# Scores in one product of 128 keys, and the forward table built ahead of the first casts: a windowed attention and spectral-mixing kernel on one core

## The chip, the cores and the metric

The kernel runs on one NeuronCore of a Trainium2 chip. The core has five engines that run side by side, each with its own instruction stream: TensorE (PE in the profile; its weight loads have a row of their own, PEld), VectorE (DVE), ScalarE (ACT), GpSimd (POOL) and SyncE (SP). Transfers between HBM and the on-chip memory SBUF are carried by 16 DMA engines; here they are issued by GpSimd, which can also cast float32 to bfloat16 on the way, and by SyncE. Matrix products land in PSUM, a small memory of eight banks.

The metric is the device time of one launch in microseconds (us); lower is better. Three runs of the kernel before took 447.45, 447.73 and 449.92 us, so the median is 447.73 us.

## What is computed

The reference has two parts, one fed into the other:

```python
# attention: batch 8, heads 8, seq 576, head_dim 64, window 64
scores = scale * np.matmul(q, k.transpose(0, 1, 3, 2))
rel = pos[:, None] - pos[None, :]
scores = np.where((rel >= 0) & (rel < 64), scores, -1000000000.0)
attn = softmax(scores)                      # max taken off first
x = np.matmul(attn, v)                      # then to [8, 576, 512]

# spectral mixing: the 64 lowest modes of a real FFT over the sequence
X = np.fft.rfft(x, axis=1)[:, :64]
Yr = einsum('bmd,mde->bme', Xr, w_r) - einsum('bmd,mde->bme', Xi, w_i)
Yi = einsum('bmd,mde->bme', Xr, w_i) + einsum('bmd,mde->bme', Xi, w_r)
u = x + np.fft.irfft(Y, n=576, axis=1)
out = u + np.maximum(u @ w_ch, 0.0)
```

A query sees itself and the 63 keys before it. So a block of 64 queries, number n, needs only the 128 keys of blocks n - 1 and n, and block 0 only its own 64. Each of the 64 modes has its own 512 x 512 matrices w_r and w_i, float32 in HBM; they are cast to bfloat16 by the DMA that loads them.

## The kernel before

**Stages.** The attention of all batches runs first and takes up the time to about 195 us. Meanwhile GpSimd already loads the weights of the modes, as far as there is room, and the first ten groups of four modes are multiplied for half of the features (`early_step`, L454). Then the remaining modes are multiplied as their weights arrive, while TensorE fits in the product of x and w_ch. A last stage brings the modes back to positions and writes the output.

**Attention.** A group g is four heads of one batch; there are 16. For each, q, k and v arrive as [128, 18, 64] tiles `rawq`, `rawk`, `rawv` (two buffers each). `transpose_raw` (L208) turns half a tile by 18 small transposes on TensorE into a PSUM tile `tr`, and ScalarE copies that to `qT`, `kT` or `vT` (L218). The `tr` tiles, and the tiles `vb` of `place_v`, share two PSUM buffers. `place_v` (L221) transposes v back, so that keys lie on partitions, and writes it into `vd` by VectorE: slot n of `vd` holds the 128 key rows that block n needs, in the order in which the columns of its scores stand. Odd slots are written from PSUM (L229), the even ones are put together out of the odd ones (L232, L233).

**Units.** 40 units of up to eight tiles [128 x 128] follow one another in a software pipeline (loop at L467, `it` from -3 to 42). `do_s` (L246) starts a PSUM tile `s` of four score tiles with the mask (L253, a product with the identity), adds the products of q and k, and takes the row maximum on VectorE (L271). `do_exp` takes the maximum off with one more product (L279) and exponentiates on ScalarE (L281); `do_pt` transposes the result (L287), and `do_pv` multiplies it with `vd` (L307) and divides by the row sum.

In `do_s`, an odd block n has its 128 keys in the order previous, own, which is the order in `kT`, and takes one product of 128 columns (L261). An even block has them in the order own, previous, and takes two products of 64 columns (L264, L267); block 0 takes only its own. Each product has its own weight load. The mask `mask_t` has three layouts: [0] for units with an even and an odd block, [1] the same with nothing before block 0, [2] for units that hold block 8 alone.

**Order of the loads.** GpSimd issues in program order. The loads of k and q of group g + 2 (L201) wait until the transposes of the group before in that buffer are done; the loads of weights (L155) stand between them, and how many are issued in each step is fixed by `due(it)` (L451).

**The start.** SyncE loads k and q of group 0 without a cast, and VectorE casts them (L348). GpSimd makes the identity (masks.py), loads v of group 0, and after two iotas the loads of group 1, two more iotas (`at`, L369 and L371), and the first weights. VectorE makes the masks and, behind them, the argument of the forward table (cosines and sines for the transform to modes): seven steps on [128 x 384] (L400 to L407). ScalarE takes the sine, between two loads of its function tables (Sin, then Exp), in step `it` = -1 (`forward_table`, L410; called at L478), after the first six copies of `tr`. Q, R and `at` lie in a tile (`XQ`) that is used for weights and modes later. The table `trigF` is first read by the transforms of step 7 (`do_dft`).

Of the kernel before, what the change touches and what calls it, by code (L numbers as in the profile page):

```python
# [11 lines left out]
BF16 = mybir.dt.bfloat16  # L12

ALU = mybir.AluOpType
ACT_F = mybir.ActivationFunctionType
# [5 lines left out]
NEG = -1.0e30  # L21
# [5 lines left out]
def kernel(  # L27
# [10 lines left out]
    nc = tc.nc  # L38
    B, H, S, D = q.shape
# [26 lines left out]
    ident = consts.tile([128, 128], FP32, name="ident")  # L66
    ident_bf = consts.tile([128, 128], BF16, name="ident_bf")
# [111 lines left out]

    with tc.manual_schedule():  # L180
        maskp = pool("maskp")
        mask_t = maskp.tile([128, 3, 4, 128], BF16, name="mask_t")
        rawp = pool("rawp", bufs=2)
        qtp = pool("qtp", bufs=3)
        vtp = pool("vtp")
# [11 lines left out]
        def load(g, nm):  # L197
            hb, b = divmod(g, B)
            src = {"q": q, "k": k, "v": v}[nm][b, 4 * hb:4 * hb + 4]
            r = rawp.tile([128, TP, D], BF16, name="raw" + nm, tag="raw" + nm)  # L200
            nc.gpsimd.dma_start(out=r, in_=src.rearrange("h (p j) d -> (h p) j d", j=TP))  # L201
            raws[g, nm] = r
# [18 lines left out]
        def place_v(g, pr):  # L221
            vd, t = Vd[g % NVD], turned[g, "v"][:, pr]
            pt = ps_m.tile([128, NTC, 2, D], BF16, name="vb", tag="misc")
            for c in range(NTC):
                n = min(128, S - 128 * c)
                nc.tensor.transpose(out=pt[0:n, c].rearrange("p h d -> p (h d)"), in_=t[:, 128 * c:128 * c + n],  # L226
                                    identity=ident_bf)
            hd = slice(pr, 4, 2)
            nc.vector.tensor_copy(out=vd[:, 1:9:2, hd, 0:D], in_=pt[:, 0:4])  # L229
            nc.vector.tensor_copy(out=vd[0:64, 8, hd, 0:D], in_=pt[0:64, 4])  # L230
            if pr:
                nc.vector.tensor_copy(out=vd[0:64, 0:8:2, :, 0:D], in_=vd[0:64, 1:9:2, :, 0:D])  # L232
# [13 lines left out]
        def do_s(u, c2):  # L246
            g0, cc, tl = units[u]
            if c2 >= len(tl) // 4:
                return
            s = ps_s.tile([128, 4, 128], FP32, name="s")  # L250
            st[u]["s", c2] = s
            mk = 2 if cc == 2 else (1 if (cc == 0 and c2 == 0) else 0)
            nc.tensor.matmul(out=s, lhsT=ident_bf, rhs=mask_t[:, mk], start=True, stop=True)  # L253
            for t, g, pr, n in tl[4 * c2:4 * c2 + 4]:
                t -= 4 * c2
                qT, kT = turned[g, "q"][:, pr], turned[g, "k"][:, pr]
                for hh in range(2):
                    ro = slice(64 * hh, 64 * hh + 64)
                    lq = qT[ro, 64 * n:64 * n + 64]
                    if n % 2:  # L260
                        nc.tensor.matmul(out=s[ro, t, :], lhsT=lq, rhs=kT[ro, 64 * n - 64:64 * n + 64],  # L261
                                         start=False, stop=True, skip_group_check=True)
                    else:
                        nc.tensor.matmul(out=s[ro, t, 0:64], lhsT=lq, rhs=kT[ro, 64 * n:64 * n + 64],  # L264
                                         start=False, stop=True, skip_group_check=True)
                        if n:
                            nc.tensor.matmul(out=s[ro, t, 64:128], lhsT=lq, rhs=kT[ro, 64 * n - 64:64 * n],  # L267
                                             start=False, stop=True, skip_group_check=True)
# [90 lines left out]
        nc.gpsimd.iota(Pcol, pattern=[[0, 1]], base=0, channel_multiplier=1,  # L359
                       allow_small_or_imprecise_dtypes=True)  # L360
        nc.gpsimd.iota(Kf, pattern=[[1, 64]], base=0, channel_multiplier=0,
                       allow_small_or_imprecise_dtypes=True)
        for nm in ("k", "q", "v"):
            load(1, nm)
        scratch = XQ[1].rearrange("p s b m -> p (s b m)").bitcast(FP32)
        Q = scratch[:, 0:NTF * 2 * NM].rearrange("p (c a m) -> p c a m", c=NTF, a=2)
        R = scratch[:, NTF * 2 * NM:3 * NTF * NM].rearrange("p (c m) -> p c m", c=NTF)
# [2 lines left out]
                       allow_small_or_imprecise_dtypes=True)  # L370
        nc.gpsimd.iota(at[:, NTC:NTF], pattern=[[0, 1]], base=128 * (NTC - 1) - 64, channel_multiplier=1,  # L371
                       allow_small_or_imprecise_dtypes=True)
        LEAD = 4
# [6 lines left out]
        ve.tensor_single_scalar(out=Gcol, in_=Pcol, scalar=64.0, op=ALU.is_ge)  # L380
        ve.scalar_tensor_tensor(out=Mcol, in0=Gcol, scalar=-64.0, in1=Pcol, op0=ALU.mult, op1=ALU.add)
        curm = mask_t[:, 0, 0, 0:64]
        prvm = mask_t[:, 0, 0, 64:128]
        ve.tensor_scalar(out=curm, in0=Kf, scalar1=Mcol, scalar2=NEG, op0=ALU.is_gt, op1=ALU.mult)
        ve.tensor_scalar(out=prvm, in0=Kf, scalar1=Mcol, scalar2=NEG, op0=ALU.is_le, op1=ALU.mult)
        for f in casts:
            f()
        for i in range(NVD):
            nc.gpsimd.memset(Vd[i][:, :, :, D:D + 1], 1.0)
            nc.gpsimd.memset(Vd[i][64:128, 0, :, :], 0.0)  # L390
        ve.tensor_copy(out=mask_t[:, 0, 1, 0:64], in_=prvm)
        ve.tensor_copy(out=mask_t[:, 0, 1, 64:128], in_=curm)
        ve.tensor_copy(out=mask_t[:, 0, 2:4, :], in_=mask_t[:, 0, 0:2, :])
        ve.tensor_copy(out=mask_t[:, 1], in_=mask_t[:, 0])
        ve.memset(mask_t[:, 1, 0:4:2, 64:128], NEG)
        ve.tensor_copy(out=mask_t[:, 2, 0:4:2, :], in_=mask_t[:, 0, 0:4:2, :])
        ve.tensor_copy(out=mask_t[:, 2, 1:4:2, :], in_=mask_t[:, 0, 0:4:2, :])
        ve.tensor_copy(out=ident_r, in_=ident)
        turns = Q[:, :, 1, :]
        ve.scalar_tensor_tensor(out=turns, in0=Kf.unsqueeze(1).to_broadcast([128, NTF, NM]), scalar=1.0 / S,  # L400
                                in1=at.unsqueeze(2).to_broadcast([128, NTF, NM]), op0=ALU.mult, op1=ALU.mult)
# [5 lines left out]
        ve.tensor_scalar(out=turns, in0=turns, scalar1=-PSAFE / (2.0 * np.pi), scalar2=PSAFE / (2.0 * np.pi),  # L407
                         op0=ALU.max, op1=ALU.min)

        def forward_table():  # L410
            nc.scalar.preload_act_table(ACT_F.Sin)
            nc.scalar.activation(out=trigF.rearrange("p c (a m) -> p c a m", a=2), in_=Q, func=ACT_F.Sin,
                                 scale=-2.0 * np.pi)
            nc.scalar.preload_act_table(ACT_F.Exp)

        def trig_steps():
            yield lambda: ve.memset(trigF[64:128, NTC - 1, :], 0.0)
# [49 lines left out]
        for it in range(-3, NU + 3):  # L467
            todo = tq.get(it, [])
            reshape(todo[0:1])
            if 0 <= it < NU:  # L470
                do_exp(it)
            if 0 <= it + 1 < NU:
                do_s(it + 1, 0)
            reshape(todo[1:2])
            if 0 <= it + 1 < NU:
                do_s(it + 1, 1)
            if it == -1:
                forward_table()  # L478
# [12 lines left out]
            reshape(todo[3:])  # L491

            g = starts.get(it + 2)
            if g is not None and g + 2 < NG:
                load(g + 2, "k")
                load(g + 2, "q")
            g = starts.get(it + 1)
            if g is not None and g + 2 < NG:
                load(g + 2, "v")
            if it >= 0:  # L500
                for f in trig[0:2]:
                    f()
                del trig[0:2]
            load_weights(due(it) - loaded())
# [338 lines left out]
```

## Time and profile before

| | us |
|---|---|
| median of three runs (447.45 to 449.92) | 447.73 |
| the profiled execution, its own time | 445.86 |
| its span, from the first to the last instruction | 444.1 |

| engine | busy us | share of the span |
|---|---|---|
| TensorE products | 337.2 | 76% |
| TensorE weight loads | 217.6 | 49% |
| VectorE | 216.3 | 49% |
| ScalarE | 173.8 | 39% |
| GpSimd | 143.4 | 32% |

The profile comes from one execution that a hardware profiler recorded. A row of a group or of the timeline has the line of the kernel, the engine and operation, what is written and read (out<-in, by tile names) and the size. In the timeline the first two numbers are the start from the begin of the span and the duration; a bracket at the end says how long the engine had stood idle before and what released it. In the chain of waits the work that ended last is followed back, at each step to what released it; "issue" there and as a releaser means that nothing in the profile explains the wait. "Granted clock" is the share of TensorE's full clock that it was given in a stretch. The share of the DMA engines can go over 1.00, since the times of packets overlap a little. A busy TensorE isn't TensorE at its peak, since its products overlap.

### The profile page before, as it was taken

What the parts mean: (1) busy time and instruction counts of PE and PEld (TensorE: products, weight loads), DVE (VectorE), ACT (ScalarE), POOL (GpSimd) and SP (SyncE); (2) the same over time, 40 slices, a digit from 0 to 9 for tenths busy, and PEclk for the clock granted to TensorE, in tenths of its full rate; (3) what the DMA queues carried; (4) which work ended last, traced back from release to release, by engine and by line L of the source; (5) the groups of instructions that cost most, each with busy time, mean ns of one, the idle gap of its engine ahead of it and who ended that gap; (6) DMA issues with size and microseconds to landing.
All of it is one profiled execution on the core that took longest, in us unless ns stands there. A gap on an engine that the chain in (4) does not pass through costs nothing.

```text
span 444.1 us, 11428 instructions
## 1 busy us (share of the span) xinstructions
PE 337.2 (76%) x4926; PEld 217.6 (49%) x4968; DVE 216.3 (49%) x448; ACT 173.8 (39%) x305; POOL 143.4 (32%) x211
## 2 busy tenths in 40 slices
PE   7687988888899988896317555775778576698994
PEld 4466766665676756674114222443344343353552
DVE  5576777765667666677204111212123122344773
ACT  4665756564575756641202100111122121123662
POOL 9242423221425243232232323132233222300773
PEclk9899999998999999999758656869889968889998
DMA  8999999999999999999999999999999999992787
GB/s 211 210 211 211 212 212 209 211 211 211 170 211 148 210 211 211 211 212 211 211 258 211 211 211 211 211 211 211 211 211 211 211 211 211 211 197 61 268 297 270
DMA packets 47875, 93.48 MB, mean 211 GB/s; under 512 B 3536, under 2 KB 3664, under 8 KB 47824
## 3 DMA queue, kind: packets, MB, share of 16 engines
q0 software_dynamic: 42000, 81.73, 98.1%
q1 hardware_dynamic: 5824, 11.01, 7.3%
q8 instruction: 39, 0.64, 0.5%
q14 instruction: 12, 0.10, 0.1%
HBM read 163.58 MB, written 9.44 MB: 390 GB/s over the span
## 4 chain that ended last, share of the span: by engine, by line
PE 41%; DMA 40%; issue 10%; ACT 4%; POOL 1%; DVE 1%; DVEq 0%; SPq 0%; POOLq 0%; ACTq 0%
DMA wr<-in_moe_w_r_dram 36%; PE tr L214 7%; PE s L279 4%; PE pt L287 4%; PE vb L226 4%; PE s L264 3%; DMA wi<-in_moe_w_i_dram 3%; PE o L307 3%; PE s L253 2%; PE psm L171 2%; PE s L261 2%; DMA vd<-in_q_dram 1%; PE px L330 1%; ACT vT L218 1%; POOL wi L155 1%
## 5 line engine op out<-in xcount | busy, mean ns | idle before, releaser
L593 PE MATMUL psz<-wch,tr 128*128 128x512 f32 x176 | 65.4, 505 | 11.0 <-DMA wch<-in_moe_w_ch_dram 11.0
L669 DVE CAST xw<-psz 128x512 fp32r<-128x512 f32 x36 | 24.9, 692 | 95.7 <-PE psz L593 94.2
L155 POOL DMA_DIRECT2D wi<-in_moe_w_i_dram x62 | 44.1, 712 | 84.4 <-PE psm L171 57.3
L271 DVE TENSOR_REDUCE mx<-s 128x4 fp32r<-128x512 f32 x72 | 49.7, 691 | 35.8 <-PE s L261 29.7
L171 PEld LDWEIGHTS <-XQ 128*32 128x32 bf16 x512 | 23.6, 168 | 84.9 <-issue 78.5
L155 POOL DMA_DIRECT2D wr<-in_moe_w_r_dram x53 | 38.1, 718 | 76.0 <-PE psm L171 37.5
L570 ACT CAST tr<-ptx 128x512 fp32r<-128x512 bf16 x36 | 21.2, 588 | 101.5 <-PE ptx L586 101.5
L171 PE MATMUL psm<-wi,XQ 128*32 128x512 bf16 x244 | 32.6, 451 | 34.1 <-DMA wi<-in_moe_w_i_dram 34.1
L593 PEld LDWEIGHTS psz<-wch,tr 128*128 128x128 f32 x176 | 38.6, 243 | 17.4 <-issue 11.3
L171 PE MATMUL psm<-wr,XQ 128*32 128x512 bf16 x212 | 29.0, 468 | 23.0 <-DMA wr<-in_moe_w_r_dram 22.3
L281 ACT ACTIVATE p<-s 128x512 bf16<-128x512 f32 x72 | 39.8, 604 | 15.2 <-PE s L279 15.2
L218 ACT COPY kT<-tr 128x576 bf16<-128x576 bf16 x32 | 23.2, 724 | 29.4 <-PE tr L214 29.4
L264 PE MATMUL s<-kT,qT 64*64 64x64 bf16 x320 | 25.7, 204 | 8.1 <-issue 8.1
L201 POOL DMA_DIRECT2D rawk<-in_k_dram x15 | 8.3, 555 | 70.3 <-PE tr L214 70.3
L768 POOL TENSOR_TENSOR ut<-ut,XQ 128x512 f32<-128x512 f32 x16 | 20.6, 1285 | 28.1 <-DVE ut L752 21.8
L218 ACT COPY qT<-tr 128x576 bf16<-128x576 bf16 x32 | 23.3, 729 | 11.0 <-PE tr L214 11.0
L290 DVE COPY pts<-pt 128x1024 bf16<-128x1024 bf16 (+1 forms) x40 | 25.3, 632 | 3.7 <-PE pt L287 1.9
L279 PE MATMUL s<-mx,ident_r 128*128 128x512 f32 x72 | 26.9, 447 | 0.0
L218 ACT COPY vT<-tr 128x576 bf16<-128x576 bf16 x32 | 23.3, 730 | 7.0 <-PE tr L214 6.9
L261 PE MATMUL s<-kT,qT 64*64 64x128 bf16 x256 | 23.6, 225 | 2.7 <-issue 2.7
L264 PEld LDWEIGHTS <-qT 64*64 64x64 bf16 x320 | 15.5, 109 | 20.7 <-issue 20.3
L287 PE MATMUL pt<-ident_bf,p 128*128 128x128 bf16 x288 | 23.0, 220 | 0.2 <-DVE pts L290 0.2
(180 smaller groups left out, 630.0 us busy)
## 6 DMA issues: line engine op xcount, KB each, us to landing
wi<-in_moe_w_i_dram POOLq DMA_DIRECT2D x60, 512.0 KB, 15.7
wr<-in_moe_w_r_dram POOLq DMA_DIRECT2D x53, 512.0 KB, 16.4
out_dram<-ut SPq DMA_DIRECT2D x32, 256.0 KB, 2.3
rawv<-in_v_dram POOLq DMA_DIRECT2D x16, 288.0 KB, 11.1
rawk<-in_k_dram POOLq DMA_DIRECT2D x15, 288.0 KB, 9.4
rawq<-in_q_dram POOLq DMA_DIRECT2D x15, 288.0 KB, 9.8
Ypair<-in_moe_w_r_dram POOLq DMA_DIRECT2D x5, 512.0 KB, 12.7
x_sb<-in_moe_w_r_dram POOLq DMA_DIRECT2D x4, 512.0 KB, 12.4
```

The lines of the kernel that those rows point to most:

```text
L155: nc.gpsimd.dma_start(out=w[:, 0:len(ps)], in_=src[ps[0]:ps[-1] + 1, HALF * hb:HALF * hb + HALF, :].rearrange("g (p j) e -> p g j e", j=NJ))
L171: nc.tensor.matmul(out=psm[32 * g:32 * g + 32, :], lhsT=XQ[hb].rearrange("k s b m -> k (s b) m")[:, (3 * j + 1 - ri) * B:(3 * j + 5 - ri) ...
L214: nc.tensor.transpose(out=pt[ro, j, :], in_=raw[ro, TH * half + j, :], identity=ident_bf[ro, ro])
L218: nc.scalar.copy(out=to, in_=pt.rearrange("p j n -> p n j"))
L261: nc.tensor.matmul(out=s[ro, t, :], lhsT=lq, rhs=kT[ro, 64 * n - 64:64 * n + 64], start=False, stop=True, skip_group_check=True)
L264: nc.tensor.matmul(out=s[ro, t, 0:64], lhsT=lq, rhs=kT[ro, 64 * n:64 * n + 64], start=False, stop=True, skip_group_check=True)
L271: nc.vector.tensor_reduce(out=mx, in_=s, axis=AX.X, op=ALU.max, negate=True)
L279: nc.tensor.matmul(out=s, lhsT=ident_r, rhs=mx.unsqueeze(2).to_broadcast([128, 4, 128]), start=False, stop=True, skip_group_check=True)
L281: nc.scalar.activation(out=p[:, 4 * c2:4 * c2 + 4, :], in_=s, func=ACT_F.Exp, scale=EX_SCALE)
L287: nc.tensor.transpose(out=pt[:, t, :], in_=st[u]["p"][:, t, :], identity=ident_bf)
L290: nc.vector.tensor_copy(out=ps[:, 0:nt, :], in_=pt[:, 0:nt, :])
L593: nc.tensor.matmul(out=pz, lhsT=tr[:, c, :], rhs=wch[:, c, :], start=(c == 0), stop=(c == NDCH - 1))
```

## The change

- Scores: every block n > 0 takes one product of 128 columns, keys in the order previous, own. Block 0 writes columns 64 to 127. 256 products and their 256 weight loads go.
- v: the even slots of `vd` are put together with their halves exchanged, so the copies move rows from partitions 0 to 63 to 64 to 127, and the other way. The zeros for the block before the first one stand in the lower half.
- Masks: one order for all units, so two layouts in place of three, and fewer steps to make them.
- Forward table: its iotas (Kf and the two of `at`) stand first on GpSimd, ahead of the identity and of all loads; its seven steps stand first on VectorE, ahead of the casts of k and q, with the cast of the identity among them; the sine with its two loads of function tables stands ahead of the first copy on ScalarE, and no longer in step -1.
- The masks and `ident_r` are made behind the casts.

```diff
-        mask_t = maskp.tile([128, 3, 4, 128], BF16, name="mask_t")
+        mask_t = maskp.tile([128, 2, 4, 128], BF16, name="mask_t")
...
-            nc.vector.tensor_copy(out=vd[0:64, 8, hd, 0:D], in_=pt[0:64, 4])
+            nc.vector.tensor_copy(out=vd[64:128, 8, hd, 0:D], in_=pt[0:64, 4])
             if pr:
-                nc.vector.tensor_copy(out=vd[0:64, 0:8:2, :, 0:D], in_=vd[0:64, 1:9:2, :, 0:D])
-                nc.vector.tensor_copy(out=vd[64:128, 2:9:2, :, 0:D], in_=vd[64:128, 1:9:2, :, 0:D])
+                nc.vector.tensor_copy(out=vd[64:128, 0:8:2, :, 0:D], in_=vd[0:64, 1:9:2, :, 0:D])
+                nc.vector.tensor_copy(out=vd[0:64, 2:9:2, :, 0:D], in_=vd[64:128, 1:9:2, :, 0:D])
...
-            mk = 2 if cc == 2 else (1 if (cc == 0 and c2 == 0) else 0)
+            mk = 1 if cc == 0 and c2 == 0 else 0
...
-                    if n % 2:
-                        nc.tensor.matmul(out=s[ro, t, :], lhsT=lq, rhs=kT[ro, 64 * n - 64:64 * n + 64],
-                                         start=False, stop=True, skip_group_check=True)
-                    else:
-                        nc.tensor.matmul(out=s[ro, t, 0:64], lhsT=lq, rhs=kT[ro, 64 * n:64 * n + 64],
-                                         start=False, stop=True, skip_group_check=True)
-                        if n:
-                            nc.tensor.matmul(out=s[ro, t, 64:128], lhsT=lq, rhs=kT[ro, 64 * n - 64:64 * n],
-                                             start=False, stop=True, skip_group_check=True)
+                    lo = 64 if n == 0 else 0
+                    nc.tensor.matmul(out=s[ro, t, lo:128], lhsT=lq, rhs=kT[ro, 64 * n - 64 + lo:64 * n + 64],
+                                     start=False, stop=True, skip_group_check=True)
...
         casts = list(load_by_sp(0, "k", Vflat[1])) + list(load_by_sp(0, "q", Vflat[2]))
-        masks.make_identity(nc, ident)
-        load(0, "v")
-        nc.gpsimd.iota(Pcol, ...)
         nc.gpsimd.iota(Kf, ...)
-        for nm in ("k", "q", "v"):
-            load(1, nm)
...
         nc.gpsimd.iota(at[:, 0:NTC], ...)
         nc.gpsimd.iota(at[:, NTC:NTF], ...)
+        masks.make_identity(nc, ident)
+        load(0, "v")
+        nc.gpsimd.iota(Pcol, ...)
+        for nm in ("k", "q", "v"):
+            load(1, nm)
         LEAD = 4
         load_weights(LEAD)
...
-        ve.tensor_copy(out=ident_bf, in_=ident)
-        (Gcol, Mcol, curm, prvm, the casts, the copies of the masks, ident_r)
         ve.scalar_tensor_tensor(out=turns, ...)
         ve.tensor_scalar(out=R, in0=turns, scalar1=MAGIC, scalar2=None, op0=ALU.add)
+        ve.tensor_copy(out=ident_bf, in_=ident)
...
-        def forward_table():
-            nc.scalar.preload_act_table(ACT_F.Sin)
-            nc.scalar.activation(out=trigF..., in_=Q, func=ACT_F.Sin, scale=-2.0 * np.pi)
-            nc.scalar.preload_act_table(ACT_F.Exp)
+        nc.scalar.preload_act_table(ACT_F.Sin)
+        nc.scalar.activation(out=trigF..., in_=Q, func=ACT_F.Sin, scale=-2.0 * np.pi)
+        nc.scalar.preload_act_table(ACT_F.Exp)
+        (Gcol, Mcol)
+        for f in casts:
+            f()
+        (the ones and zeros of vd, by GpSimd)
+        ve.tensor_copy(out=ident_r, in_=ident)
+        (the masks: curm, prvm, three copies, one memset)
...
-            if it == -1:
-                forward_table()
```

More of the change, by code (lines that the diff above doesn't have):

```diff
@@ L408 @@
                          op0=ALU.max, op1=ALU.min)
-        def forward_table():
[L411 to L414, printed above, removed]
+        nc.scalar.preload_act_table(ACT_F.Sin)
+        nc.scalar.activation(out=trigF.rearrange("p c (a m) -> p c a m", a=2), in_=Q, func=ACT_F.Sin,
+                             scale=-2.0 * np.pi)
+        nc.scalar.preload_act_table(ACT_F.Exp)
+        ve.tensor_single_scalar(out=Gcol, in_=Pcol, scalar=64.0, op=ALU.is_ge)
+        ve.scalar_tensor_tensor(out=Mcol, in0=Gcol, scalar=-64.0, in1=Pcol, op0=ALU.mult, op1=ALU.add)
+        for f in casts:
+            f()
+        for i in range(NVD):
+            nc.gpsimd.memset(Vd[i][:, :, :, D:D + 1], 1.0)
+            nc.gpsimd.memset(Vd[i][0:64, 0, :, :], 0.0)
+        ve.tensor_copy(out=ident_r, in_=ident)
+        prvm, curm = mask_t[:, 0, 0, 0:64], mask_t[:, 0, 0, 64:128]
+        ve.tensor_scalar(out=curm, in0=Kf, scalar1=Mcol, scalar2=NEG, op0=ALU.is_gt, op1=ALU.mult)
+        ve.tensor_scalar(out=prvm, in0=Kf, scalar1=Mcol, scalar2=NEG, op0=ALU.is_le, op1=ALU.mult)
+        ve.tensor_copy(out=mask_t[:, 0, 1, :], in_=mask_t[:, 0, 0, :])
+        ve.tensor_copy(out=mask_t[:, 0, 2:4, :], in_=mask_t[:, 0, 0:2, :])
+        ve.tensor_copy(out=mask_t[:, 1], in_=mask_t[:, 0])
+        ve.memset(mask_t[:, 1, 0:4:2, 0:64], NEG)
         def trig_steps():
```

23 lines of the change are left out of this document (2 added, 21 removed).

## The prediction, made before the changed kernel had run

> **What bounds the kernel now.** I read the page first, then the busy time by stages with the DMA rate, then the order of time on GpSimd, and last the chain of waits through the first 30 us.
>
> ```profile
> span 444.1 us, 11428 instructions
> PE 337.2 (76%) x4926; PEld 217.6 (49%) x4968; DVE 216.3 (49%) x448; ACT 173.8 (39%) x305; POOL 143.4 (32%) x211
> q0 software_dynamic: 42000, 81.73, 98.1%
> q8 instruction: 39, 0.64, 0.5%
> ```
>
> No engine is full, but the queue of the loads that GpSimd issues is: its packets take 98.1% of all 16 DMA engines. So the question is where those engines run dry. The stages show it (columns: stretch, its length, busy time and count of PE, PEld, DVE, ACT, POOL, then granted clock, DMA share, GB/s):
>
> ```profile
> 15.00:20.00 5.00, 3.10 (x25) 1.79 (x25) 1.55 (x4) 3.14 (x5) 0.00 (x0) 0.74 1.12 209
> 105.00:110.00 5.00, 4.62 (x75) 3.22 (x69) 2.46 (x6) 2.53 (x4) 0.00 (x0) 0.66 1.12 211
> 110.00:120.00 10.00, 8.62 (x189) 6.37 (x190) 6.70 (x17) 5.79 (x12) 4.46 (x7) 1.00 1.00 165
> 134.00:145.00 11.00, 10.50 (x238) 7.56 (x241) 8.44 (x21) 6.30 (x12) 5.89 (x9) 1.00 0.89 146
> 145.00:195.00 50.00, 45.29 (x1044) 33.72 (x1053) 33.68 (x74) 30.54 (x55) 15.54 (x23) 1.00 1.12 211
> 195.00:387.00 192.00, 121.81 (x857) 67.91 (x858) 52.59 (x99) 33.53 (x61) 53.64 (x75) 0.78 1.12 214
> ```
>
> The rate is 211 GB/s nearly everywhere up to the last weight, whatever the engines do, and 165 and 146 GB/s in two holes. The holes cost 10 x (211 - 165)/211 = 2.2 us and 11 x (211 - 146)/211 = 3.4 us: 5.6 us in which the stream stood. After 145 us it never stands again, and the last weights end the stage:
>
> ```profile
> 388.28 13.64 DMA wi<-in_moe_w_i_dram
> ```
>
> They land at 401.9 us; what follows is untouched by the change. So the end moves only by what the two holes lose or gain. GpSimd makes the holes:
>
> ```profile
> 124.17 0.56 POOL L201 DMA_DIRECT2D rawk<-in_k_dram  x1 [7.30 <-PE tr L214]
> ...
> 136.30 0.53 POOL L201 DMA_DIRECT2D rawk<-in_k_dram  x1 [6.46 <-PE tr L214]
> ```
>
> Each load of k waits until TensorE has transposed the previous k out of that buffer, and the weights are queued behind it. When TensorE is late in the attention stage, GpSimd issues late, and the DMA engines empty what they had. If TensorE is earlier by some lead at 111 and 136 us, these issues come earlier by it, while the stream that begins at 1 to 2 us is the same. The time lost is then 5.6 us minus the lead, not below nothing. So I sum the lead.
>
> **The forward table's sine, moved ahead of the copies: 2.6 us of lead.** In the chain of waits ScalarE holds TensorE up, because the two table loads and the sine stand ahead of a copy of k that frees a PSUM buffer:
>
> ```profile
> 12.30 1.28 ACT L411
> 13.60 0.84 ACT trigF L412
> 14.46 1.28 ACT L414
> 15.75 0.73 ACT kT L218
> 16.52 0.56 PE vb L226 x5
> ...
> 12.41 0.69 PE L214 MATMUL tr<-ident_bf,rawk 64*64 64x64 bf16 x18
> ```
>
> Without the three, the copy waits only for its transposes, until 12.41 + 0.69 = 13.10. It ends at 13.85 and vb starts at 13.9 instead of 16.52: 2.6 us.
>
> What they pass on the way costs something at the start:
>
> ```profile
> 0.74 0.20 POOL masks.py:197 MEMSET ident<- 128x128 f32 x1 [0.29 <-POOLq L827]
> 1.20 5.17 DMA vd<-in_q_dram
> 3.96 0.19 POOL L369 IOTA XQ<- 128x5 f32 x1
> 5.03 0.94 DVE L348 CAST rawk<-vd 128x576 bf16<-128x576 f32 x2 [1.83 <-DMA vd<-in_k_dram]
> 6.35 0.72 ACT L218 COPY kT<-tr 128x576 bf16<-128x576 bf16 x1 [4.33 <-PE tr L214]
> 7.74 0.67 PE L214 MATMUL tr<-ident_bf,rawk 64*64 64x64 bf16 x18
> 9.44 0.54 DVE L400 SCALAR_TENSOR_TENSOR XQ<-Kf,XQ 128x384 f32<-128x384 f32 x1
> 12.30 0.36 DVE L407 TENSOR_SCALAR XQ<-XQ 128x384 f32<-128x384 f32 x1
> ```
>
> On GpSimd three iotas of at most 0.2 us go ahead of the identity and the first loads, so v's first load is issued some 0.4 us later and the weights, behind all of it in both kernels, not at all. That is hidden: k and q, by SyncE, keep the DMA engines full till 6.37. On VectorE the seven table steps took 9.44 to 12.66, 3.2 us. From about 1.3 (0.74 plus the iotas) with the identity's cast and two one-column steps (an estimate: 0.2 each, from the 0.36 of L407) they end near 5.2, against 5.03 for k's first cast: 0.2 us late. ScalarE's sine then runs at about 4.9 and Exp's table is in at 7.0, so the first copy of k comes 0.65 later than 6.35 and ends at 7.7. Its buffer is wanted by the next transposes of k, which start at 7.74 behind q's, and q lands at 6.37 anyway: cost 0, with 0.05 us of cover; a later table costs its whole delay. I allow 0 to 1.5 us. The masks, now shorter by three copies, end near 9.6 and are wanted at 9.96.
>
> **The half-clock stretch after that pause: 1.0 us.** In 15 to 20 us the granted clock is 0.74, so 1.3 us of clock is missing right behind TensorE's 2.9 us pause. With the pause gone I take 1.0 (TensorE is busy 3.10 of those 5 us, so not all of it counts); bounds 0 and 1.7, the latter from 105 to 110, where (1 - 0.66) x 5 is missing.
>
> **One product of 128 keys: 0.4 us.** A warm block of scores:
>
> ```profile
> 24.10 0.22 PE L264 MATMUL s<-kT,qT 64*64 64x64 bf16 x2
> 24.15 0.20 PE L267 MATMUL s<-kT,qT 64*64 64x64 bf16 x2
> 24.18 0.23 PE L261 MATMUL s<-kT,qT 64*64 64x128 bf16 x2
> 24.24 0.20 PE L264 MATMUL s<-kT,qT 64*64 64x64 bf16 x2
> ```
>
> From start to start a pair of 64 columns takes 0.03 to 0.05 and a pair of 128 takes 0.06: the streaming is equal, and only the odd 0.00 to 0.02 per block is saved. Some 50 of the 72 blocks stand ahead of 136 us: 0 to 1.0, I take 0.4.
>
> **512 fewer PE instructions: 0.6 us.** 4926 + 4968 instructions in 39 transfers of q8 are 254 for each, so two transfers go. TensorE pauses in the middle of equal transposes, with nothing to wait for:
>
> ```profile
> PE tr L214 <- issue: 5.8, 6, 1.8
> ```
>
> I read these as instructions not yet there, about 1 us each; not every transfer has one. Two transfers fewer, three quarters of them ahead of 136 us: 0 to 2.9 (1.5 x 1.9) better, and up to 1 worse since the pauses fall elsewhere; I take 0.6. The Trainium skill (Runtime: NRT & Kernel Launch, Instruction fetch mechanics) says that fetching is mostly hidden; by that rule this term is 0 and the lead 4.0. The pauses inside one group speak against it here.
>
> **v, placed to match: 0.** The copies now move 64 partitions up or down:
>
> ```profile
> L232 DVE COPY vd<-vd 64x1024 bf16<-64x1024 bf16 x16 | 6.7, 418 | 0.0
> L794 DVE CAST zst<-psz 128x512 fp32r<-128x512 f32 x1 | 0.7, 692 | 1.4 <-PE psz L788 1.4
> L800 DVE CAST Z<-psp 16x512 fp32r<-16x512 f32 x1 | 0.7, 682 | 0.5 <-PE psp L799 0.5
> ```
>
> L800 writes rows 96 to 111 from rows 0 to 15 and costs what L794 does in place. So the count is the same and I take no change; at worst, at L800's 1.33 ns per element, a copy costs 1.37 instead of 0.42, all on VectorE, which is idle over a quarter of this stage. The Trainium skill (VectorE: DVE Perf Modes, Two Vector instructions with no wait between them) says that an instruction whose output starts in another 32-partition group than the last is held until all earlier ones end; by it these copies lose an overlap that is under 0.1 us each, off the path, and the sum stays.
>
> **Sum.** 2.6 + 1.0 + 0.4 + 0.6 = 4.6 us of lead at 136 us, so the holes keep 1.0 of their 5.6 us. The loads allow that lead at their tightest place:
>
> ```profile
> rawk<-in_k_dram POOLq DMA_DIRECT2D x15, 288.0 KB, 9.4
> 21.44 0.55 POOL L201 DMA_DIRECT2D rawk<-in_k_dram  x1 [8.22 <-PE tr L214]
> 35.48 0.45 PE L214 MATMUL tr<-ident_bf,rawk 64*64 64x64 bf16 x18
> ```
>
> 21.44 + 9.4 = 30.8 is 4.6 us ahead of its use, where the lead is 3.6 to 3.8. The profiled execution took 445.86 us (span 444.1 and 1.76 around it) and would take 441.3; the median of the runs is 1.87 above it, so 447.73 - 4.6 = 443.1.
>
> **Rivals.** *All of both holes goes:* the half-clock stretch at 105 to 110, behind another pause, doesn't recur; the lead grows by up to 1.7 and the gain stops at 5.6: 442.1. For it: the pauses move. Against: some pause may fall as badly. The Trainium skill (TensorE: Matmul & The Clock Gate, Part 1) says that the clock is judged in free-running windows, so chance decides; that is why this stays a rival. *The lead is spent:* TensorE, now earlier, catches up with its loads, pauses there, and gets two half-clock stretches of 1.7 us ahead of 136 us: 4.6 - 3.4 = 1.2, so 446.5. For it: only 0.8 to 1.0 us of margin at that k. Against: in the rows the wait runs the other way, GpSimd for TensorE. *Slower, by the table at the start:* the VectorE steps, beside GpSimd's descriptors and memsets, take three times 3.2 us. The first cast waits 6.4 us more, all attention with it, and 6.6 - 4.6 = 2.0 us is lost: 449.7. It decides once the steps take over 3.2 + 4.4 = 7.6 us. Against: at 9.44 they ran beside four loads' issues too. *The merged product saves nothing:* 443.5, inside the forecast.
>
> **How the numbers follow.** Forecast 0.48, all holes gone 0.18, lead spent 0.20, slower 0.14. About 0.5%, 2.2 us, can be told from no change here: below 445.5 is faster, above 450.0 slower by it; under the last case I count the worse starts too. Faster: 0.44 + 0.18 + 0.04 = 0.66; same: 0.04 + 0.15 + 0.02 = 0.21; slower: 0.01 + 0.12 = 0.13. The range goes from 441.3 (all gone, less 0.8 for scatter) to 447.6 (lead spent, plus 1.1); the likeliest alone has 442.1 to 444.8.
>
> **What would show it.** Right: first vb near 13.9 us; no clock below 0.9 in 15 to 20; over 200 GB/s in the first hole and over 190 in what is left of the second; last weights at about 397.3; span near 439.5. Wrong in a step: the first copy of k after 7.7; score blocks of the same length but more pauses between; copies of v over 0.5 us; TensorE waiting for DMA ahead of transposes. Wrong altogether: the holes filled and the end not moved, or the lead there and the holes as deep.

## The result, and the profile after

| | before | after |
|---|---|---|
| median of the runs, us | 447.59 (446.12 to 449.92, 4 runs) | 442.51 (441.96 to 443.10, 4 runs) |
| the profiled execution, its own time | 445.86 | 441.96 |
| its span | 444.1 | 440.2 |
| last weights land | 401.92 | 397.02 |

The ratio of the times is 0.9882, with a 95% interval from 0.9837 to 0.9927: 5.1 us less from median to median, where the prediction had 4.6. The two profiled executions stand 3.9 us apart. The rest is scatter of the kernel before: its median lies 1.7 us above its profiled execution, that of the changed kernel 0.55 above.

The head of the page of the changed kernel, in the same rows as before:

```profile
span 440.2 us, 10911 instructions
PE 330.7 (75%) x4670; PEld 211.8 (48%) x4712; DVE 219.8 (50%) x445; ACT 172.8 (39%) x304; POOL 143.3 (33%) x211
q0 software_dynamic: 42000, 81.73, 98.4%
q8 instruction: 37, 0.61, 0.5%
```

The same bytes in the load queue, 256 products and 256 weight loads fewer, and two instruction transfers fewer. The stages of the changed kernel (stretch, length, busy time and count of PE, PEld, DVE, ACT, POOL, granted clock, DMA share, GB/s):

```profile
1.00:8.00 7.00, 4.15 (x30) 1.49 (x32) 6.74 (x15) 3.49 (x4) 6.86 (x16) 1.00 0.90 237
15.00:20.00 5.00, 4.39 (x63) 2.65 (x63) 2.90 (x8) 1.68 (x4) 0.20 (x1) 0.63 1.12 211
105.00:110.00 5.00, 3.95 (x77) 2.93 (x71) 2.50 (x5) 2.78 (x8) 1.95 (x3) 1.00 1.12 211
110.00:120.00 10.00, 9.52 (x213) 6.91 (x218) 7.20 (x15) 6.56 (x12) 3.24 (x5) 1.00 1.12 212
134.00:145.00 11.00, 10.61 (x266) 8.54 (x269) 7.48 (x15) 8.15 (x17) 3.71 (x6) 1.00 1.12 211
383.00:397.00 14.00, 10.56 (x59) 5.24 (x59) 4.46 (x8) 2.34 (x4) 0.83 (x2) 0.90 0.88 164
394.00:402.00 8.00, 7.03 (x21) 2.62 (x21) 1.38 (x2) 0.64 (x2) 0.00 (x0) 0.57 0.14 26
```

And the stretches of the kernel before that stand against the first and the last two of them: the start, the same 14 us ahead of the last landing, and the 8 us around it:

```profile
1.00:8.00 7.00, 5.04 (x54) 2.35 (x56) 3.64 (x12) 1.77 (x3) 6.73 (x15) 1.00 0.90 243
388.00:402.00 14.00, 11.37 (x64) 6.66 (x62) 4.46 (x8) 2.34 (x4) 0.83 (x2) 0.82 0.91 171
398.00:406.00 8.00, 5.18 (x26) 2.05 (x21) 1.57 (x3) 0.83 (x2) 0.00 (x0) 1.00 0.20 38
```

Both holes are gone altogether: 212 and 211 GB/s where 165 and 146 stood. That is the whole 5.6 us. Three smaller things take some of it back:

- The stream starts a little later: 237 against 243 GB/s from 1 to 8 us, which is 6 x 7 / 211 = 0.2 us.
- It thins out a little more at its end: 164 against 171 GB/s in the 14 us ahead of the last landing, 7 x 14 / 211 = 0.5 us. So the last weights land 5.6 - 0.2 - 0.5 = 4.9 us earlier, which is what the chain of waits of the changed kernel shows:

```profile
383.28 13.74 DMA wi<-in_moe_w_i_dram
397.07 1.01 PE psm L171 x2
```

- From there to the end it takes 440.2 - 397.0 = 43.2 us instead of 42.2. The products behind the last weights take 1.01 us where they took 0.61, since the granted clock from 394 to 402 us is 0.57; in the kernel before it is 1.00 around its last landing.

5.6 - 0.2 - 0.5 - 1.0 = 3.9 us, the distance of the two spans.

**The lead of TensorE** is read at the loads of k on GpSimd, which wait for its transposes. The rows that stood at 111.36 and 136.30 us before are, in the timeline of the changed kernel:

```profile
102.61 0.55 POOL L201 DMA_DIRECT2D rawk<-in_k_dram  x1 [2.95 <-PE tr L214]
127.25 0.53 POOL L201 DMA_DIRECT2D rawk<-in_k_dram  x1 [5.90 <-PE tr L214]
```

They are 8.8 and 9.0 us earlier, twice the 4.6 that were forecast. The start doesn't give this. The chain of waits of the changed kernel at its place:

```profile
13.80 0.73 ACT kT L218
14.58 0.83 PE vb L226 x5
```

vb starts at 14.58 instead of 16.52, 1.9 us earlier. The other 7 us come later, in the attention loop. What TensorE waits for there can be read in the view of waits: the releaser, then total us, count and longest. First the kernel before, from 20 us to the load of k at 136; then the changed kernel from 18 us to the same load at 127 (three rows with a named releaser, 1.8 us in all and the same in both, are left out):

```profile
PE tr L214 <- issue: 5.5, 5, 1.8
PE s L264 <- issue: 4.5, 26, 0.4
PE vb L226 <- issue: 1.0, 1, 1.0
PE s L261 <- issue: 1.0, 2, 0.6
PE o L307 <- issue: 0.9, 1, 0.9
```

```profile
PE s L261 <- issue: 4.1, 25, 0.3
PE tr L214 <- issue: 1.7, 4, 0.9
PE pt L281 <- issue: 1.3, 2, 0.8
PE vb L226 <- PE o L301: 0.7, 1, 0.7
PE vb L226 <- issue: 0.2, 1, 0.2
```

The rows marked "issue" sum to 12.9 and 7.3 us. The many short ones, 0.16 us each ahead of a product of q and k, are nearly alike in both (4.5 and 4.1 us). The few long ones, for which the profile names nothing that TensorE waited for, have shrunk. The row of 0.7 us that the profile puts down to a product belongs with them: this pause, at 43.87 us, sits where the long ones sit, 510 recorded instructions behind the one at 31.79 us (see below). With it the pauses went from 12.9 to 8.0 us, 4.9 us less. With 1.9 from the start, and 1.7 from the half clock at 105 to 110 us that didn't come back (0.66 before, 1.00 now), less 0.5 for 15 to 20 us, where it is 0.63 instead of 0.74, that makes 8.0 of the 9.0 us; the last 1.0 us isn't accounted for.

### The profile page after: what moved, and what is told of

Its sections match the earlier page's. It is cut to its first block, busy times and chain, and to the rows that moved or that the text cites. A ratio compares the mean times of both kernels' runs of the same rounds, so it can differ in the third digit from the quotient of the medians.

```text
span 440.2 us, 10911 instructions
## 1 busy us (share of the span) xinstructions
PE 330.7 (75%) x4670; PEld 211.8 (48%) x4712; DVE 219.8 (50%) x445; ACT 172.8 (39%) x304; POOL 143.3 (33%) x211
## 4 chain that ended last, share of the span: by engine, by line
DMA 42%; PE 40%; issue 8%; DVE 3%; ACT 3%; POOL 1%; DVEq 0%; POOLq 0%
DMA wr<-in_moe_w_r_dram 35%; PE tr L214 6%; PE s L261 5%; PE s L273 4%; PE pt L281 4%; PE vb L226 4%; DMA rawk<-in_k_dram 4%; DMA wi<-in_moe_w_i_dram 3%; PE psm L171 3%; PE o L301 3%; PE s L253 2%; PE psm L720 1%; PE px L324 1%; PE pst L746 1%; PE psz L720 1%
## 5 line engine op out<-in xcount | busy, mean ns | idle before, releaser
L579 PE MATMUL psz<-wch,tr 128*128 128x512 f32 x176 | 61.4, 480 | 11.0 <-DMA wch<-in_moe_w_ch_dram 11.0
L171 PE MATMUL psm<-wi,XQ 128*32 128x512 bf16 x244 | 34.2, 453 | 39.9 <-DMA wi<-in_moe_w_i_dram 39.9
L171 PE MATMUL psm<-wr,XQ 128*32 128x512 bf16 x212 | 27.9, 448 | 27.3 <-DMA wr<-in_moe_w_r_dram 26.7
L579 PEld LDWEIGHTS psz<-wch,tr 128*128 128x128 f32 x176 | 35.9, 226 | 16.8 <-issue 11.2
L261 PE MATMUL s<-kT,qT 64*64 64x128 bf16 (+1 forms) x576 | 29.4, 223 | 6.9 <-issue 6.9
L261 PEld LDWEIGHTS <-qT 64*64 64x64 bf16 x576 | 18.0, 108 | 18.4 <-issue 17.9
L598 DVE TENSOR_TENSOR stg<-psm,Ypair 128x512 bf16<-128x512 f32 x10 | 6.9, 690 | 35.1 <-PE psm L171 35.1
L313 DVE TENSOR_TENSOR x_sb<-o,r 128x512 bf16<-128x512 f32 x32 | 22.1, 691 | 1.1
```

What stands on the lines that cost most here:

```text
L171: nc.tensor.matmul(out=psm[32 * g:32 * g + 32, :], lhsT=XQ[hb].rearrange("k s b m -> k (s b) m")[:, (3 * j + 1 - ri) * B:(3 * j + 5 - ri) ...
L261: nc.tensor.matmul(out=s[ro, t, lo:128], lhsT=lq, rhs=kT[ro, 64 * n - 64 + lo:64 * n + 64], start=False, stop=True, skip_group_check=True)
L579: nc.tensor.matmul(out=pz, lhsT=tr[:, c, :], rhs=wch[:, c, :], start=(c == 0), stop=(c == NDCH - 1))
```

## What the long pauses are: the question for the experiments

The packets of the instruction queue (q8) that fall into attention begin, taken from the two traces, at

```
before  60.2 66.2 72.1 78.1 84.0 90.0 96.0 102.4 108.3 113.5 121.5 127.5 133.4 137.2 144.1
after   59.4 65.3 71.3 77.2 83.2 89.3 95.2 101.0 107.1 113.4 119.7 125.7 131.6 137.9 143.8
```

and carry 16 KB each, by the prediction's division some 254 PE instructions. They come 5.8 to 6.1 us apart nearly everywhere, whatever TensorE runs. In the stretch from 20 to 140 us the view of DMA counts for the kernel before

```profile
q8 instruction: 20, 0.33, 1.0%
```

and the same 20 for the changed one, and TensorE's own row there is, before and after,

```profile
20.00:140.00 120.00, 104.75 (x2540) 0.98 1.09 203
```

```profile
20.00:140.00 120.00, 109.58 (x2507) 1.00 1.12 211
```

About the same number of products in the same time, though those of the second are longer. With as many weight loads that is 42 instructions per us, and 254 in 5.95 us is 43. So the reading is: while the DMA engines are full of loads, TensorE gets its next block of instructions only every 5.95 us, and a stage with many small instructions goes at that pace. 512 instructions fewer in the 195 us of attention are then 512 / 42 = 12 us of supply, not the 0.6 of the prediction. This is theory F in the expectations below. Against it stands the prediction's own reading, that the start brings most of the lead and fetching next to nothing, and as a third the possibility that the new place of v and the masks bring it.

## The experiments

### The scores alone

The kernel before, with the one product per block, v and the masks as in the change, and the old start:

```diff
...
+                    lo = 64 if n == 0 else 0
+                    nc.tensor.matmul(out=s[ro, t, lo:128], lhsT=lq, rhs=kT[ro, 64 * n - 64 + lo:64 * n + 64], ...)
...
-                nc.vector.tensor_copy(out=vd[0:64, 0:8:2, :, 0:D], in_=vd[0:64, 1:9:2, :, 0:D])
+                nc.vector.tensor_copy(out=vd[64:128, 0:8:2, :, 0:D], in_=vd[0:64, 1:9:2, :, 0:D])
...
             if it == -1:
                 forward_table()
...
```

> The kernel before with the merged product, the v placement and the two masks; the start is that of before. Theory F (TensorE's instructions arrive in blocks of 256, one each 5.94 us, and that paces the attention stage): at the 13th group the lead of TensorE over the kernel before is some 9.0 - 1.8 = 7.2 us, which is over the 5.6 us of both holes, so both are gone and the time is that of the changed kernel, 442.5 +- 0.7. The terms of the prediction (blocks of scores 0.4, fetching 0.6): lead 1.0, holes keep 4.6 us, 446.6. A rival, that the start alone made it: 447.6.

Measured: 442.07 us (440.97 to 442.71, 6 runs) beside 447.75 for the kernel before (445.20 to 451.34, 20 runs); ratio 0.9866, interval 0.9827 to 0.9906. The start is the old one: the chain of waits has vb at 16.94. Its two holes:

```profile
110.00:120.00 10.00, 9.22 (x187) 6.97 (x193) 6.20 (x14) 6.37 (x13) 2.72 (x5) 1.00 1.12 210
134.00:145.00 11.00, 10.61 (x234) 8.05 (x229) 7.43 (x18) 7.20 (x15) 3.32 (x5) 1.00 1.11 210
```

The scores alone fill both holes. The pauses from 20 to 130 us are row by row those of the changed kernel (4.1, 1.7, 1.3, 0.7 and 0.2 us), and the load of k at 136.30 is issued at 129.35: 7.0 us of lead that begins at nothing, where theory F had 7.2. This part is worth the whole gain.

### The start alone

The changed kernel with the scores, v and masks of the kernel before (of the edit, the scores alone are shown):

```diff
...
-                    lo = 64 if n == 0 else 0
-                    nc.tensor.matmul(out=s[ro, t, lo:128], ...)
+                    if n % 2:
+                        nc.tensor.matmul(out=s[ro, t, :], ...)
+                    else:
+                        nc.tensor.matmul(out=s[ro, t, 0:64], ...)
+                        if n:
+                            nc.tensor.matmul(out=s[ro, t, 64:128], ...)
...
```

> The changed kernel with the scores, v and the three masks of before. Theory F: lead 1.8 us from the start and nothing after it, holes keep 3.8 of 5.6 us, stream begins 0.3 later: 446.1 +- 0.7. The terms of the prediction (2.6 + 1.0): lead 3.6, holes keep 2.0: 444.0. A rival, that the start alone made it: 442.5.

Measured: 443.81 us (442.36 to 446.82, 12 runs), ratio 0.9917 (0.9890 to 0.9944). The stages:

```profile
15.00:20.00 5.00, 4.15 (x94) 2.87 (x97) 3.38 (x10) 3.30 (x7) 1.07 (x2) 1.00 1.12 210
110.00:120.00 10.00, 8.62 (x173) 6.22 (x175) 6.56 (x15) 5.28 (x12) 3.33 (x5) 1.00 1.12 211
130.00:145.00 15.00, 13.45 (x304) 9.84 (x308) 11.62 (x28) 8.85 (x16) 5.89 (x9) 1.00 1.00 175
```

The load of k at 136.30 is issued at 133.30: a lead of 3.0 us. Three loads of k earlier, at 95.04 instead of 98.11, it is the same, so it doesn't grow. The first hole is filled. The second, which the lead has moved forward, keeps 15 x (211 - 175)/211 = 2.6 us: 5.6 us less the lead, as the prediction's rule has it. The time is that of the prediction's own terms, 444.0, and not theory F's 446.1, since the start gives more than F had allowed for it: vb is at 14.58 here too, 1.9 us earlier, and the half clock from 15 to 20 us (0.74 before) isn't there, which gives the 1.3 us that the prediction had counted as 1.0. The changed kernel had the half clock in that place again (0.63). That the time agrees with 444.0 is in part luck: the holes gave 3.0 us, and the two profiled executions lie only 1.8 us apart (445.86 and 444.05). The prediction's first two terms, 3.6 us together, came out at 3.0 (the lead) to 3.2 (1.9 + 1.3) in this run, and at 1.9 - 0.5 = 1.4 in the profiled run of the changed kernel. The pauses are those of the kernel before: 12.8 us against 12.9.

### The new layout, with two products of 64 in even blocks

The changed kernel, with v, masks and start as they are, and the even blocks in two adjacent products of 64 columns, so that only the number of PE instructions is as before:

```diff
-                    nc.tensor.matmul(out=s[ro, t, lo:128], lhsT=lq, rhs=kT[ro, 64 * n - 64 + lo:64 * n + 64], ...)
+                    wd = 64 if n and n % 2 == 0 else 128 - lo
+                    for c in range(lo, 128, wd):
+                        nc.tensor.matmul(out=s[ro, t, c:c + wd], lhsT=lq,
+                                         rhs=kT[ro, 64 * n - 64 + c:64 * n - 64 + c + wd], ...)
```

> The changed kernel, but each even block takes its 128 keys in two products of 64 adjacent columns: the layout, v placement, masks and start of after, the number of PE instructions of before (9438 rows in the program instead of 8926). Theory F: as with the start alone, lead 1.8, 446.1 +- 0.7, with pauses of 1 to 2 us at each second or third block of 256 instructions again. If it was the order of keys, the masks or the v placement: 442.5.

Measured: 443.66 us (442.43 to 445.03, 9 runs), ratio 0.9905 (0.9872 to 0.9938): the time of the start alone. It lies between the two expectations, theory F's 446.1 having too little for the start again, and its interval overlaps that of the changed kernel (0.9837 to 0.9927), so the time by itself decides nothing. The trace does: the load of k is issued at 132.60, a lead of 3.7 us instead of 9.0, and the waits for issue up to 133 us sum to 11.8 us. So v's place and the masks bring at most the 0.7 us of lead that this kernel has beyond the start alone. Since a warm group of scores takes 0.43 us here and 0.41 in the changed kernel (rows in the sections below), the merged product has its worth from the number of instructions. How the pauses go with that number is seen in the timeline of TensorE. This kernel, then the one with the start alone, at the same transposes of v:

```profile
77.01 0.29 PE L214 MATMUL tr<-ident_bf,rawv 64*64 64x64 bf16 x8
78.22 0.34 PE L214 MATMUL tr<-ident_bf,rawv 64*64 64x64 bf16 x10 [0.93 <-issue]
```

```profile
76.36 0.29 PE L214 MATMUL tr<-ident_bf,rawv 64*64 64x64 bf16 x8
77.58 0.34 PE L214 MATMUL tr<-ident_bf,rawv 64*64 64x64 bf16 x10 [0.93 <-issue]
```

In both, and in the kernel before (0.93 us at 79.45), TensorE stops behind the 8th of 18 equal transposes, whose data has long been there, and goes on with the 9th 0.93 us later. In each of the three it is the same instruction, by count, and up to 2.8 us apart in time. The changed kernel has fewer instructions ahead of these transposes and runs through them:

```profile
81.99 0.45 PE L214 MATMUL tr<-ident_bf,rawv 64*64 64x64 bf16 x18
85.51 0.45 PE L281 MATMUL pt<-ident_bf,p 128*128 128x128 bf16 x5 [0.48 <-issue]
```

Its pause comes at 85.51 us, behind other work. So the place is bound to the count of instructions and not to the time, the layout or the kind of work. Listed from 30 to 110 us in the five kernels so far and in the next one, the pauses of over 0.3 us which end in "issue" are 254 to 256 recorded PE instructions apart, or two to four times that, and TensorE goes on 1.2 to 1.5 us after a transfer of q8 has ended. Three pauses of under 0.4 us don't fit: at 108.91 us before, at 105.66 with the start alone, at 48.13 in the next kernel.

### Twice as many small products

The same with `wd = 32`: four products in an even block, 512 products and weight loads more than the kernel before.

```diff
-                    wd = 64 if n and n % 2 == 0 else 128 - lo
+                    wd = 32 if n and n % 2 == 0 else 128 - lo
```

> As the one before, but four products of 32 columns: 1024 rows more than the kernel before, some 690 of them ahead of the second hole. Theory F: 690 x 5.94 / 256 = 16 us later there, less 1.8 from the start: lead -14, the holes grow by about that, 461 +- 4. If only the streaming of columns counts (0.12 instead of 0.06 us for a block's pair, 86 pairs ahead of the hole): lead -3, 450.6.

Measured: 457.10 us in the profiled run, so without an interval; a second run took 465.51 us. 457.10 is the lower edge of what theory F had (461 +- 4) and 6.5 us above what streaming alone had. The load of k at 136.30 is issued at 146.19, 9.9 us late, where F had 14 and streaming 3. But the kernel doesn't separate the theories as cleanly as was meant. In the timeline of this kernel, and of the one with two products of 64, a warm group of four score tiles with what follows it:

```profile
17.35 0.58 PE L263 MATMUL s<-kT,qT 64*64 64x32 bf16 x20
17.74 0.47 PE L214 MATMUL tr<-ident_bf,rawk 64*64 64x64 bf16 x18
```

```profile
17.60 0.43 PE L263 MATMUL s<-kT,qT 64*64 64x64 bf16 x12
17.86 0.45 PE L214 MATMUL tr<-ident_bf,rawk 64*64 64x64 bf16 x18
```

From its start to the next work the group takes 0.39 us instead of 0.26: products of 32 columns are not only more, they stream worse. The load of k that has 124.17 us before is issued at 132.15 here and at 120.63 with two of 64: 11.5 us apart. Some 45 of the 72 groups stand ahead of it (an estimate, from the 50 ahead of 136 us), so 45 x 0.13 = 6 us are the products themselves. The waits for issue add some 3 (15.2 us to 146 us, against 11.8 to 133), with one of 1.5 at 45.77 us that the profile puts down to VectorE though it sits at a block's edge, and a half clock stretch (0.83 from 110 to 120) 1.7. What does speak for theory F is the pace, TensorE's row of this kernel from 20 to 140 us:

```profile
20.00:140.00 120.00, 103.03 (x2579) 0.96 1.06 195
```

The number of products in 120 us is once more the same within the few per cent of records that can be missing, and q8 has its 20 transfers.

### Warmth at the end, and the first load first

The losses at the start and at the end can be attacked alone. Seven products of 512 columns that nobody reads stand ahead of the last weights' products; and the load of v of group 0 stands ahead of the three iotas. The first alone, the second alone, both, and both on top of the scores alone (which has the old order on GpSimd otherwise):

```diff
+                if (grp, hb) == steps[-1] and ri:
+                    fill = bank("z")
+                    for _ in range(7):
+                        nc.tensor.matmul(out=fill, lhsT=ident_bf, rhs=trigI[:, 0:DM], start=True, stop=True)
```

```diff
+        load(0, "v")
         casts = list(load_by_sp(0, "k", Vflat[1])) + list(load_by_sp(0, "q", Vflat[2]))
...
         masks.make_identity(nc, ident)
-        load(0, "v")
```

> The changed kernel with seven more products of 128x512 (identity with the inverse table, into a free PSUM bank, never read) ahead of the last half group's w_i part, where TensorE waits 1.8 us for weights. They add work that the reference doesn't need. Theory: from the last weight to the end the kernel before took 42.2 us, the changed one 43.1 (44.0 in the run with the scores alone), because TensorE, waiting for the thinning stream, is put to half clock from 394 to 401 us. With the wait filled the half-clock stretch goes or moves, and that part is 42.2 or less: 441.5 +- 0.7. Rival (the stretch has nothing to do with the wait, or the added products delay the last group): 442.5 to 443.5.

> The changed kernel with the first load of v ahead of the iotas and the identity on GpSimd. Theory: the stream of loads ran 0.25 to 0.3 us later than before over its whole length, since GpSimd began it 0.45 us later, and 0.2 earlier than before with the scores alone; now it begins some 1.1 us earlier than in the changed kernel and runs 0.5 to 1.0 us ahead of it; the table is 0.8 us later and the lead some 8 instead of 9 us, still over 5.6: 441.8 +- 0.7. Rival (the engines are full with k and q by SyncE anyway): stream and time as in the changed kernel, 442.5.

> Both of the two before: 440.9 +- 0.7 if both theories hold, 442.5 if neither.

> The scores alone on the start of before, with the filled wait and the first load of v ahead of everything. Lead 6.9 us as with the scores alone, enough for both holes: 440.7 +- 0.7, no slower than with the new start. If the 2 us of lead from the new start are worth something: 442 or more.

| | median us | runs | ratio (95%) | span | last weights land |
|---|---|---|---|---|---|
| before, beside them | 446.54 | 446.00 to 447.69, 7 | | | |
| warm end | 441.31 | 441.24 to 441.63, 4 | 0.9879 (0.9861 to 0.9897) | 439.9 | 397.55 |
| first load first | 441.81 | 441.54 to 442.61, 4 | 0.9894 (0.9876 to 0.9912) | 440.0 | 397.84 |
| both | 441.45 | 441.21 to 441.91, 4 | 0.9884 (0.9867 to 0.9900) | 439.4 | 397.26 |
| scores alone, and both | 440.98 | 440.80 to 441.23, 4 | 0.9873 (0.9857 to 0.9888) | 439.0 | 396.82 |

The warm end does what it should in the trace. Its chain of waits, and its stretch around the last landing:

```profile
384.19 13.36 DMA wi<-in_moe_w_i_dram
397.59 0.60 PE psm L171 x2
```

```profile
394.00:402.00 8.00, 6.30 (x27) 2.46 (x25) 1.63 (x3) 1.16 (x2) 0.00 (x0) 1.00 0.19 36
```

The clock is full there, and from the last weights to the end it takes 439.9 - 397.55 = 42.3 us instead of 43.2. But the kernel with only the first load moved has no products added and takes 440.0 - 397.84 = 42.2: the half clock simply didn't fall there in that run. So the filled wait removes a loss that comes and goes, and in the times the medians put it at 0.4 us (441.81 to 441.45), less than the intervals can tell.

The first load first missed what was expected of the stream, though its time is the 441.8 that was forecast. GpSimd then begins the iotas 1.2 us later, VectorE's table with them (its first step starts at 2.44 instead of 1.22), and the first copy of k moves from 7.66 to 8.32; in the bytes of the queue the stream is only 0.1 us earlier than in the changed kernel (2.970 against 2.950 MB by 20 us).

All four medians lie inside what was expected, but the kernel before, beside them, is itself 1.05 us faster than beside the changed kernel. So it is the ratios that count, and by these nothing is gained: 0.9873 to 0.9894 here, 0.9882 for the changed kernel, 0.9866 for the scores alone without either addition, with intervals that overlap. The last row has the lowest median and the lowest span, and isn't shown to be faster than any of them, but it does without the new start. The load of k at 136.30 is issued at 125.46, 126.19, 127.47 and 129.04 in the four, leads of 10.8, 10.1, 8.8 and 7.3 us, and the least of them goes with the lowest time: once the merged product fills the holes, more lead has nothing left to fill.

## Why the prediction was right, point by point

- **What bounds the kernel, and by what the gain is capped: right.** The stream of loads sets the end, the holes were worth 5.6 us, and both went. Of the four cases it was "all of both holes goes" that happened, with 442.1; the likeliest one had kept 1.0 us of the second hole. The time lies between the two. The rule that the holes keep 5.6 us minus the lead was tested where the lead is smaller: 3.0 us left 2.6 (the start alone), and 3.7 left 1.3 instead of 1.9 (two products of 64, 193 GB/s from 130 to 145 us).
- **512 fewer PE instructions, 0.6 us: mis-sized, and the largest term of all.** The pauses shrank by 4.9 us up to the second hole, both with the new start and with the old one, and came back where the number of instructions was put back: 12.8 us with the start alone, 11.8 with two products of 64, against 12.9 before and 8.0 after. The prediction had read the pauses rightly as instructions that are not yet there. It took them as two transfers saved, with one pause of 1 us for each, where it is the pace that counts: each block has its 5.95 us, and the pauses are only what is left of it when TensorE has run the block faster than that. Its upper bound for this term, 2.9 us, was too low for the same reason.
- **The sine ahead of the copies, 2.6 us: 1.9.** vb came at 14.58 instead of 13.9. Two steps of VectorE at the start were long, in the timeline:

```profile
4.09 1.37 DVE L382 TENSOR_SCALAR XQ<-XQ 128x384 f32<-128x384 f32 x1
5.63 1.72 DVE L342 CAST rawk<-vd 128x576 bf16<-128x576 f32 x2
7.66 0.72 ACT L218 COPY kT<-tr 128x576 bf16<-128x576 bf16 x1
7.92 0.47 PE L214 MATMUL tr<-ident_bf,rawq 64*64 64x64 bf16 x18 [1.25 <-DVE rawq L342]
```

  The last step of the table took 1.37 us where 0.36 had been seen (L407), and k's two casts, from 5.63, took 1.72 where 0.94 had been seen (L348); why they did was not tried. TensorE was late in two ways at once. The transposes of q, behind the casts, came at 7.92 instead of 7.24, and this is the way that the chain of waits takes. The first copy of k, behind the sine, began at 7.66, so it ended at 8.38 where the prediction's limit for its end was 7.7. Both are the 0.7 us that vb is late. The prediction's allowance of 0 to 1.5 us holds; its value of 0 doesn't.
- **The half clock behind that pause, 1.0 us: right once, wrong once.** With the start alone it was gone (1.00), in the profiled run of the whole change it was there again (0.63). The second one, at 105 to 110 us, went where the long pause ahead of it (1.57 us at 103.14 before) went, and where it stayed it came back or not: with two products of 64 the pause was 1.30 us and the clock 1.00, with the start alone 1.38 us and 0.81. The Trainium skill (TensorE: Matmul & The Clock Gate, Part 1) has the clock judged in free-running windows; these two rows fit that, since almost the same pause led to both, but they don't show it.
- **One product of 128 keys, 0.4 us of streaming: not seen apart.** A warm group took 24.10 to 24.53 us before, 0.43. The changed kernel's takes 0.41:

```profile
25.77 0.41 PE L261 MATMUL s<-kT,qT 64*64 64x128 bf16 x8
```

  That would be up to 1 us over 50 groups, but while the supply sets the pace it would only lengthen the pauses.
- **v, placed to match, 0: right.** The two big copies between halves take 431 and 455 ns instead of 418 and 433. The overlap that the prediction let them lose wasn't there before either: the second began where the first ended (42.12 and 0.42 us, then 42.55).
- **The rivals.** "The lead is spent" needed TensorE to catch up with its loads. It does so only late, in one wait of 2.02 us for k at 169 us, where the loads are already queued behind a full stream, and no hole opens. "Slower, by the table" failed at its price: the seven steps took 4.2 us (1.22 to 5.46), not 9.6.
- **Outside the sum: 1.7 us.** 0.2 at the start, 0.5 at the end of the stream and 1.0 from the clock behind it. The first had been called hidden, the other two had been called untouched. Why the stream thins a little more at its end was not tried; the last issues of GpSimd wait for TensorE's products with earlier weights in both kernels (3.73 us before, 3.51 after), so with the stream further ahead less stands queued behind it, but that is an argument only.

A lead of twice the forecast, capped by the holes, and losses outside the sum nearly cancel. So the time came out this near by luck as well: its forecast was better than that of its parts.

## What to carry to other kernels

Divide TensorE's instructions, products and weight loads together, by the length of a stage with a full DMA queue: where it comes near the 42 per us of this kernel, fewer and larger instructions are worth more than their own time, and pauses marked "issue" at a fixed count of instructions give it away. What an earlier engine is worth ends at the time that the real bound has lost to it, here 5.6 us in two holes; work that goes beyond it, as the new start does beside the merged product, brings nothing.

## What the runs showed of the hardware

The transfers of instructions share the DMA engines with the loads. In the rows of q8 above they come 5.8 to 6.1 us apart while the stream runs at 211 GB/s, and closer where it runs dry: 108.3 to 113.5 (5.2 us) and 133.4 to 137.2 (3.8 us) in the kernel before, at the edges of its holes; with four products of 32 columns, in deeper holes, 3.4 to 4.6. So TensorE's sequencer can take blocks faster than one each 5.95 us, and it is with the full stream that it gets no more. What in the queue makes it just that long was not tried, and no kernel here runs the attention without the stream. The Trainium skill (Runtime: NRT & Kernel Launch, Instruction fetch mechanics) has the instructions refilled in blocks of 16 KiB, 256 instructions each, which the rows bear out (0.33 MB in 20 transfers), and crossing a block mostly hidden; here it isn't: 4.9 us of lead hang on it up to 136 us.

This makes a chain that feeds on itself: the loads slow TensorE's instructions down, TensorE's lateness holds back the issue of the next loads, and a hole opens. In the hole a block comes sooner, but that TensorE gains by it isn't shown: in the kernel before the blocks behind the two early ones came 8.0 and 6.9 us later.
